# A fused threshold-attention and feed-forward kernel: input loads issued in smaller groups at round ends, and the first weight piece loaded and converted before the first scores

## The chip, the cores and the metric

The kernel runs on one core of one Trainium2 chip. The time is device microseconds (us) of one execution. Thirteen runs of the kernel before gave a median of 927.81 us, from 918.07 to 934.68.

## The reference

Two blocks follow each other. The first is attention with a threshold, for 8 batches of 8 heads, 576 tokens, head size 64:

```python
scores = scale * np.matmul(q, k.transpose(0, 1, 3, 2))
thresh = np.max(scores, axis=-1, keepdims=True) - tau
scores = np.where(scores >= thresh, scores, -1000000000.0)
attn = np.exp(scores - np.max(scores, axis=-1, keepdims=True))
attn = attn / (np.sum(attn, axis=-1, keepdims=True) + 1e-09)
return np.matmul(attn, v)
```

Its output, with the heads side by side, is `x` of 4608 tokens by 512. The second block computes `h = x @ w_in` (1024 wide), `h * softmax(h)`, a layer norm over the 1024 with gain `g_ln`, and `@ w_out` back to 512. The weights come in as float64, so the kernel turns their 64-bit words into float32 itself.

## The kernel before, in words

**Rounds.** The work is one long list of 144 "slots" (`NS`), 18 for each batch (`PER`). A slot scores 128 queries against 576 keys for two heads. The main loop runs one round for each slot. In round s it issues the scores of slot s on PE (`scores`, L391), their thresholds on VectorE, here DVE (`maxes`, L408), the ramp and the exponential on ScalarE, here ACT (L419, L428), and for slot s-1 the normalising on GpSimd, POOL (L438), and the block transposes on DVE (`blocks`, L450). At each even round the transposed blocks of two slots go through four DMAs `wT<-T` (L461) into the layout that the product with v wants. That product (`attend`, L486) is issued three rounds after the second of the two slots (`LAG_PV`), so two rounds after its `wT<-T`.

**Feed-forward.** When a group of 128 tokens is complete, four of the later rounds carry its two halves of `x @ w_in` (`ff_h`, L540) and of `@ w_out` (`ff_o`, L642). Between these, `ff_swap` copies parts of `u` into `V` by four DMAs (L620), and `ff_turn` transposes V into `uT` on DVE (L630) one round later; `ff_o` needs `uT`.

**Loads.** q, k and v of a batch come in two halves of four heads. `load_qk` loads the half of q and k (512 KB each; the first half also the last 64 tokens of all heads, `ends`, 128 KB for q and for k), and `load_v` the half of v (1,152 KB in five DMAs). The table `load_at` says in which round each of these is issued, and the loop issues them at the round's start. For batch b, with r = 18(b-1): first q/k half in round r+2, second in r+8, first v half in r+9, second in r+24; for batch 1 the first three are in rounds 8, 12 and 15.

**Weights.** There are 16 pieces (`piece`, 8 of `w_in`, 8 of `w_out`) of 128x512 64-bit words, 512 KB. `weight_load` issues the DMA of a raw piece (L205), `weight_a` takes exponent and top bits apart (two DVE operations, L216 and L222, and one on ACT, L221), `weight_b` builds the float32 value (three DVE operations, L236, L239, L242), and `weight_d` swaps the halves of a `w_out` piece by two DMAs (L251). Piece x is finished (`weight_b`) at the end of round x, then the load of piece x+3 is issued, and `weight_a` of piece x+1 follows. There are three raw buffers.

**The preamble** issues q and k of the first half, tau, the constants, raw pieces 0 to 2 on ACT's queue, the second half of q and k, v, `whole_pair(0)` (the transposes L264 and their copies L297 to L342 for the first pair of heads) and `weight_a(0)`.

**Order.** The order on every engine is the order of the program text. Nearly all DMAs are issued by SyncE (SP) in that order, and an instruction that waits holds up all behind it. DMA completions are counted by eight semaphores, used in turn: a DMA that takes one over waits until its former user has landed.

Of the kernel before, what the change touches and what calls it, by code (L numbers as in the profile page):

```python
# [8 lines left out]
F32 = mybir.dt.float32  # L9
# [7 lines left out]
P = 128  # L17
# [3 lines left out]
def kernel(  # L21
# [27 lines left out]
    nc = tc.nc  # L49
    B, H, S, D = q.shape  # L50
    DM, DFF = w_in.shape
    SM = 512
# [7 lines left out]
    ROWS = (slice(0, 64), slice(64, P))  # L60

    const = ctx.enter_context(tc.tile_pool(name="const", bufs=1))
    loads = ctx.enter_context(tc.tile_pool(name="loads", bufs=2))
# [24 lines left out]
    NK = S // 64  # L88

    halves = {}  # L90
    ends = {}
# [8 lines left out]
    def take(name):  # L100
        tag = pairs_free.pop(0)
        return tag, ps_mm.tile([P, 1024], F32, tag=tag, name=name)
# [13 lines left out]
        )  # L116


    def load_qk(b, hf):
        d = halves.setdefault((b, hf), {})  # L120
        hs = slice(4 * hf, 4 * hf + 4)

        if hf == 0:
            ends[b] = loads.tile([P, H, D], F32, tag="ends", name="ends")
        for nm, src, rows in (("q", q, ROWS[0]), ("k", k, ROWS[1])):
            d[nm] = loads.tile([P, 4, 4, D], F32, tag=nm, name=nm)

            parts = [slice(0, 2), slice(2, 4)] if b == 0 and hf == 0 else [slice(0, 4)]
            for x, part in enumerate(parts):
                queue = nc.scalar if nm == "k" and x + 1 < len(parts) else nc.sync  # L130
                queue.dma_start(
                    out=d[nm][:, part].rearrange("p h t d -> p h (t d)"),
                    in_=src[b, hs, 0:SM, :][part].rearrange("h (p t) d -> p h (t d)", t=4),
                )
                if hf == 0 and x == 0:
                    queue.dma_start(
                        out=ends[b][rows], in_=src[b, :, SM:S, :].rearrange("h p d -> p h d")
                    )

    def load_v(b, hf):  # L140
        d = halves.setdefault((b, hf), {})
        hs = slice(4 * hf, 4 * hf + 4)


        d["v"] = loads.tile([P, 4, NK, D], F32, tag="v", bufs=3, name="v")
        rest = v[b, hs, 0:SM, :].rearrange("h (p t) d -> p h (t d)", t=4)
        for to, rows, of in (
            (0, slice(0, P), slice(0, P)), (4, ROWS[0], ROWS[1]), (4, ROWS[1], ROWS[0])
        ):
            nc.sync.dma_start(  # L150
                out=d["v"][rows, :, to : to + 4].rearrange("p h t d -> p h (t d)"), in_=rest[of]
            )
        for rows in ROWS:
            nc.sync.dma_start(
                out=d["v"][rows, :, NK - 1], in_=v[b, hs, SM:S, :].rearrange("h p d -> p h d")
            )

    def constants():

        nc.gpsimd.memset(lim, 0.0)  # L160
        nc.scalar.activation(out=ntau, in_=lim, func=AF.Exp)
        make_identity(nc, ident)
        nc.gpsimd.memset(mhalf, -0.5)
        nc.gpsimd.memset(mone, -1.0)
        nc.gpsimd.memset(lim, -896.0 * 8388608.0)

        nc.vector.tensor_scalar(
            out=scl, in0=tau_t, scalar1=0.0, scalar2=SCALE, op0=ALU.is_ge, op1=ALU.mult  # L170
        )
        nc.vector.tensor_scalar(
            out=tau_t, in0=tau_t, scalar1=0.0, scalar2=104.0, op0=ALU.max, op1=ALU.min
        )
        nc.vector.tensor_scalar(out=ntau, in0=tau_t, scalar1=-1.0, scalar2=None, op0=ALU.mult)
# [13 lines left out]
    def piece(x):  # L189
        if x < 2 * NP:  # L190
            c, hf = divmod(x, 2)
            cols = slice(512 * hf, 512 * hf + 512)
            return w_in[P * c : P * c + P, cols], w1[:, c, cols], W_UNIT
        c = x - 2 * NP
        return w_out[P * c : P * c + P], w2[:, 2 * c], gs[:, c : c + 1]

    NW = 2 * NP + NC
    raws = {}

    def weight_load(x):  # L200
        raw = work.tile(
            [P, 512], I64 if wide else F32, tag=("xh2", "xh3", "uT")[x % 3], bufs=1, name="raw"
        )
        queue = nc.scalar if x < 3 else nc.sync
        queue.dma_start(out=raw, in_=piece(x)[0])  # L205
        raws[x] = dict(raw=raw)

    def weight_a(x):
        if not wide:
            return  # L210
        d = raws[x]
        hi = d["raw"].bitcast(I32).rearrange("p (n two) -> p n two", two=2)[:, :, 1]
        d["em"] = e, m = [
            work.tile([P, 512], I32, tag=t, bufs=n, name="em") for t, n in (("ob", 2), ("xe", 1))
        ]
        nc.vector.tensor_scalar(  # L216
            out=e, in0=hi, scalar1=20, scalar2=0x7FF,
            op0=ALU.logical_shift_right, op1=ALU.bitwise_and,
        )

        nc.scalar.activation(out=e, in_=e, func=AF.Relu, bias=lim, scale=8388608.0)  # L221
        nc.vector.tensor_scalar(  # L222
            out=m, in0=hi, scalar1=0xFFFFF, scalar2=0x100000,
            op0=ALU.bitwise_and, op1=ALU.bitwise_or,
        )

    def weight_b(x):
        d = raws.pop(x)
        _, dst, unit = piece(x)
        if not wide:  # L230
            nc.vector.tensor_scalar(out=dst, in0=d["raw"], scalar1=unit, scalar2=None, op0=ALU.mult)
            return
        words = d["raw"].bitcast(I32).rearrange("p (n two) -> p n two", two=2)
        lo, hi = words[:, :, 0], words[:, :, 1]
        e, m = d["em"]
        nc.vector.scalar_tensor_tensor(  # L236
            out=dst, in0=lo.bitcast(U32), scalar=2.0**-32, in1=m, op0=ALU.mult, op1=ALU.add
        )
        nc.vector.scalar_tensor_tensor(  # L239
            out=e, in0=hi, scalar=-(2**31), in1=e, op0=ALU.bitwise_and, op1=ALU.bitwise_or  # L240
        )
        nc.vector.scalar_tensor_tensor(  # L242
            out=dst, in0=dst, scalar=unit, in1=e.bitcast(F32), op0=ALU.mult, op1=ALU.mult
        )
# [104 lines left out]
    def whole_pair(i):  # L349
        tags, tiles = zip(take("tp"), take("tp"))  # L350
        spare = dict(enumerate(tiles), base=0, eased=i > 0)
        items = [item(i) for item in (q_item, k_item, e_item)]
        for x, (_, make, _) in zip((0, 4, 8), items):
            make(spare, x)
        for x, (_, _, keep) in zip((0, 4, 8), items):
            for r in range(2):
                keep(spare, x, r)
        pairs_free.extend(tags)
# [317 lines left out]
    PER = NS // B  # L676
# [12 lines left out]
    for i in range(NP, NPAIR):  # L689
        b, hp = divmod(i, NP)  # L690
        at = 11 + 2 * hp if i < 2 * NP - 1 else PER * (b - 1) + (6 + 3 * hp if hp < 3 else PER - 1)
# [7 lines left out]
    load_at = {}  # L699
    for b in range(1, B):  # L700
        r = PER * (b - 1)

        for at, job, hf in zip(
            (2, 8, 9) if b > 1 else (8, 12, 15), (load_qk, load_qk, load_v), (0, 1, 0)
        ):
            load_at.setdefault(r + at, []).append(lambda b=b, job=job, hf=hf: job(b, hf))
        load_at.setdefault(r + PER + 6, []).append(lambda b=b: load_v(b, 1))

    with tc.manual_schedule():
        load_qk(0, 0)  # L710
        nc.scalar.dma_start(out=tau_t, in_=tau.partition_broadcast(P))
        constants()
        for x in range(3):
            weight_load(x)
        load_qk(0, 1)
        load_v(0, 0)
        nc.sync.dma_start(out=g_rows, in_=g_ln.rearrange("(c p) -> c p", p=P))
        whole_pair(0)
        weight_a(0)


        pieces = {r: x for x, r in enumerate(range(16))}
        whole = {0: 1, 2: 2, 4: 3}
        load_at[3] = [lambda: load_v(0, 1)]

        ready = []
        rnd = 0
# [7 lines left out]
        while True:  # L735
            more = rnd < NS
            if not more and not (
# [1 line left out]
                or max([rnd - 1, *begin, *middle, *late]) >= rnd  # L739
            ):  # L740
                break
            for job in load_at.pop(rnd, []):
                job()
            for job in begin.pop(rnd, []):
                job()
            if rnd == NS:
# [59 lines left out]
            elif step == ("h", 1):  # L806
# [8 lines left out]
                at = rnd + 4 if more or not ready else rnd + 6  # L815
# [16 lines left out]
            if attending is not None:  # L832
                attend(attending)
                attended(attending)
                b, kind, hp = attending
# [5 lines left out]
                blocks(rnd - 1)  # L841
            for job in late.pop(rnd, []):
                job()
            if rnd == 3:
                gains()
            if rnd in pieces:
                x = pieces[rnd]
                weight_b(x)
                if x + 3 < len(pieces):
                    weight_load(x + 3)  # L850
                if x + 1 < len(pieces):
                    weight_a(x + 1)
            if rnd - 1 in pieces:
                weight_d(pieces[rnd - 1])
# [35 lines left out]
```

## Time and profile before

| what | value |
|---|---|
| median of 13 runs | 927.81 us |
| the profiled execution, its own time | 923.17 us |
| its span in the profile | 921.4 us |
| PE busy | 851.0 us (92%) |
| DVE busy | 679.1 us (74%) |
| ACT busy | 591.7 us (64%) |
| POOL busy | 452.2 us (49%) |
| DMA queue q1 (SP's), share of 16 engines | 71.1% |
| PE waits in L486 for `wT<-T` | 8.2 us in 5 |
| DVE waits in L630 for `V<-u` | 24.8 us in 12 |
| DVE waits in L216 for raw pieces of `w_in` | 7.4 us in 4 |

The span is cut into stretches to see which engine is full where. A timeline row has its start, its duration, engine, line, operation, result<-sources, and, in brackets, how long the engine stood idle before it and who ended the wait. SPq and ACTq rows are the issue of DMAs, not their transfer. The trace lacks some of the matmul records, so a short gap on PE with the releaser "issue" need not be a wait.

### The profile page before, as it was taken

How to read it: one execution, taken by the hardware profiler on the slowest of the kernel's cores; microseconds unless marked ns; L12 is line 12 of the kernel's file. 1: busy time of each engine (PE TensorE's matmuls, PEld its weight loads, DVE VectorE, ACT ScalarE, POOL GpSimd, SP SyncE). 2: the span in 40 equal slices, each digit the busy share in tenths (PEclk: the TensorE clock that was granted, in tenths of full speed). 3: DMA queues.
4: the chain of work that ended last, by engine and by line, in shares of the span. 5: the costliest groups of instructions: out<-in, count | busy, mean ns of one | idle time of the engine just before them, and what ended most of it. 6: DMA issues, size and time to landing. Idle time of an engine off the chain costs nothing. (4 is left out here: it accounts for less than half of the span.)

```text
span 921.4 us, 39657 instructions
## 1 busy us (share of the span) xinstructions
PE 851.0 (92%) x17089; PEld 625.2 (68%) x17089; DVE 679.1 (74%) x1306; ACT 591.7 (64%) x1240; POOL 452.2 (49%) x870
## 2 busy tenths in 40 slices
PE   5567779989899999999999999989999999999997
PEld 3335457868676666767777667867767777887555
DVE  5898968768766777777777777777767777777351
ACT  5766667757656766667667766767757676766121
POOL 2544646536555455545555555545555555555120
PEclk8778799999999999999999999999999999999999
DMA  8899869975889557976889557975879555866412
GB/s 256 199 255 244 192 138 221 223 159 128 185 171 222 120 132 185 227 156 138 190 183 227 123 131 183 232 147 122 197 166 212 134 135 124 191 142 135 93 47 47
DMA packets 95470, 154.61 MB, mean 168 GB/s; under 512 B 27192, under 2 KB 69184, under 8 KB 95296
## 3 DMA queue, kind: packets, MB, share of 16 engines
q1 hardware_dynamic: 93920, 150.12, 71.1%
q8 instruction: 134, 2.20, 1.1%
q10 hardware_dynamic: 1376, 1.97, 0.6%
q14 instruction: 40, 0.33, 0.1%
HBM read 46.14 MB, written 9.44 MB: 60 GB/s over the span
## 5 line engine op out<-in xcount | busy, mean ns | idle before, releaser
L408 DVE CUSTOM_DVE_ANT_0 w<-s_ps,tau_t 128x576 f32<-128x576 f32 x288 | 206.5, 755 | 149.1 <-PE s_ps L391 125.4
L419 ACT ACTIVATE w<-s_ps,nth 128x576 f32<-128x576 f32 x288 | 207.4, 743 | 119.3 <-DVE nth L408 95.8
L642 PE MATMUL o_ps<-w,uT 64*64 64x256 f32 x4608 | 268.6, 376 | 6.9 <-DVE uT L630 6.6
L642 PEld LDWEIGHTS o_ps<-w,uT 64*64 64x64 f32 x4608 | 219.7, 133 | 63.9 <-issue 20.8
L438 POOL TENSOR_SCALAR w<-w,sm 128x576 f32<-128x576 f32 x288 | 218.4, 770 | 14.3
L540 PE MATMUL h_ps<-w,xh 64*64 64x512 f32 x1856 | 219.2, 590 | 3.6 <-issue 3.6
L428 ACT ACTIVATE w<-w,ntau 128x576 f32<-128x576 f32 x288 | 220.3, 772 | 0.0
L450 DVE STREAM_TRANSPOSE T<-w 128x576 f32<-128x576 f32 x288 | 205.9, 751 | 5.4 <-POOL w L438 4.2
L486 PEld LDWEIGHTS pv<-wT,v 64*64 64x64 f32 x5760 | 170.7, 138 | 46.9 <-issue 26.2
L391 PE MATMUL s_ps<-kT,qT 64*64 64x64 f32 (+1 forms) x2048 | 174.0, 423 | 22.1 <-ACT w L419 20.2
L486 PE MATMUL pv<-wT,v 64*64 64x128 f32 (+1 forms) x5760 | 174.7, 266 | 13.8 <-DMA wT<-T 8.2
L540 PEld LDWEIGHTS h_ps<-w,xh 64*64 64x64 f32 x1856 | 111.6, 133 | 94.3 <-issue 65.0
L435 POOL TENSOR_SCALAR sm<-sm 128x2 f32<-128x2 f32 x144 | 35.7, 248 | 277.7 <-ACT w L428 275.0
L436 POOL TENSOR_TENSOR sm<-sm,mone 128x2 f32<-128x2 f32 x144 | 107.1, 744 | 12.0
L391 PEld LDWEIGHTS s_ps<-kT,qT 64*64 64x64 f32 x2048 | 65.3, 138 | 35.0 <-ACT w L419 26.8
L604 ACT ACTIVATE V<-u,nb,rs 128x1024 f32<-128x1024 f32 x36 | 44.7, 1241 | 53.3 <-POOL nb L594 53.3
L508 ACT COPY xh<-pv 128x256 f32<-128x256 f32 x64 | 23.9, 373 | 74.3 <-PE pv L486 74.3
L630 DVE STREAM_TRANSPOSE uT<-V 128x1024 f32<-128x1024 f32 x36 | 44.1, 1224 | 24.9 <-DMA V<-u 24.8
L428 ACT ACTIVATION_READ_ACCUMULATOR w<-w,ntau 128x1 f32 x288 | 56.9, 198 | 0.0
L562 ACT ACTIVATE u<-h_ps,hm 128x1024 f32<-128x1024 f32 x36 | 40.2, 1118 | 24.4 <-DVE hm L553 18.3
L553 DVE TENSOR_REDUCE hm<-h_ps 128x1 f32<-128x1024 f32 x36 | 43.0, 1194 | 10.9 <-PE h_ps L530 5.5
L568 DVE TENSOR_TENSOR u<-h_ps,u 128x1024 f32<-128x1024 f32 x36 | 42.8, 1190 | 10.5 <-ACT u L562 10.5
(74 smaller groups left out, 604.5 us busy)
## 6 DMA issues: line engine op xcount, KB each, us to landing
wT<-T SPq DMA_DIRECT2D x288, 288.0 KB, 5.8
V<-u SPq DMA_DIRECT2D x144, 64.0 KB, 3.8
out_dram<-ob SPq DMA_DIRECT2D x72, 128.0 KB, 2.9
v<-in_v_dram SPq DMA_DIRECT2D x16, 512.0 KB, 9.0
v<-in_v_dram SPq DMA_DIRECT2D x32, 256.0 KB, 8.2
q<-in_q_dram SPq DMA_DIRECT2D x15, 512.0 KB, 6.1
k<-in_k_dram SPq DMA_DIRECT2D x15, 512.0 KB, 7.8
raw<-in_moe_w_out_dram SPq DMA_DIRECT2D x8, 512.0 KB, 9.4
```

The source lines that it names most:

```text
L391: nc.tensor.matmul(out=ps[h][ROWS[y], ks], lhsT=lhsT, rhs=d["kT"][ROWS[h], ks], start=True, stop=True,)
L408: nc.vector.tensor_tensor_reduce(out=w, in0=ps[:, 0:S], in1=tau_t.to_broadcast([P, S]), scale=1.0, scalar=BIG, op0=ALU.add, op1=ALU.min, a ...
L419: nc.scalar.activation(out=d["w"][x], in_=d["ps"][x][:, 0:S], func=AF.Prelu, bias=d["nth"][x], scale=-1.0, alpha=1.0e30,)
L428: nc.scalar.activation(out=w, in_=w, func=AF.Exp, bias=ntau, scale=1.0, accum_out=sm[:, x : x + 1])
L436: nc.gpsimd.tensor_tensor(out=sm, in0=sm, in1=mone, op=ALU.pow)
L438: nc.gpsimd.tensor_scalar(out=w, in0=w, scalar1=sm[:, x : x + 1], scalar2=1.0, op0=ALU.mult, op1=ALU.mult)
L450: nc.vector.transpose(out=T[:, :, r, h, :], in_=w)
L486: nc.tensor.matmul(out=to, lhsT=d["v"][ROWS[u], h0 + h, m ^ 4 * u if m < 8 else m], rhs=rhs, start=m == 0, stop=m == NK - 1,)
L540: mm = nc.tensor.matmul(out=h[ROWS[y], f], lhsT=x[ROWS[r], c, ROWS[y]], rhs=w1_parts[ROWS[r], c, part ^ r], start=part == 0 and c == 0, st ...
L604: nc.scalar.activation(out=V, in_=u, func=AF.Identity, bias=nb, scale=rs)
L630: nc.vector.transpose(out=uT, in_=d["V"].rearrange("p y (m x) -> p m y x", x=32))
L642: nc.tensor.matmul(out=d["o"][ROWS[z], 512 * r : 512 * r + 256], lhsT=d["uT"][ROWS[r], m].rearrange("p y x -> p (y x)"), rhs=w2[ROWS[r], m ...
```

## The change

- The rounds in which loads are issued, and their sizes. q and k of a half are issued apart (`load_one`), and v in two parts (512 KB, then 640 KB). For batch b > 1: q in round r-1, k in r+1, second half k in r+7 and q in r+9, first v half in r+11 and r+13, second in r+21 and r+23. For batch 1: k in 7, q in 8, k in 11, q in 12, v in 13 and 15, and the second v half in 21 and 23.
- Loads are issued at the end of a round (after `blocks` and the late jobs) in place of its start.
- Raw piece 0 is the first DMA on ACT's queue, ahead of k. `weight_a(0)` and `weight_b(0)` stand before the three small DVE operations on tau (`thresholds`, split from `constants`) and before `whole_pair(0)`. Then follow `weight_a(1)` and the load of piece 3.
- In round r, piece r+1 is finished in place of piece r. So rounds 0 to 14 carry pieces, and round 15 none.

The order of instructions on PE is the same in both programs, and so is POOL's. The core of the diff:

```diff
-    def load_qk(b, hf):
+    def load_one(b, hf, nm, queue=None):
...
+    def load_qk(b, hf):
+        load_one(b, hf, "q")
+        load_one(b, hf, "k")
+
+    def load_v(b, hf, parts=(0, 1, 2)):
...
+    def thresholds():
         nc.vector.tensor_scalar(
             out=scl, in0=tau_t, scalar1=0.0, scalar2=SCALE, op0=ALU.is_ge, op1=ALU.mult
         )
...
-        for at, job, hf in zip(
-            (2, 8, 9) if b > 1 else (8, 12, 15), (load_qk, load_qk, load_v), (0, 1, 0)
+        for at, job, hf, what in (
+            (-1 if b > 1 else 8, load_one, 0, "q"),
+            (1 if b > 1 else 7, load_one, 0, "k"),
+            (7 if b > 1 else 11, load_one, 1, "k"),
+            (9 if b > 1 else 12, load_one, 1, "q"),
+            (11 if b > 1 else 13, load_v, 0, (0,)),
+            (13 if b > 1 else 15, load_v, 0, (1, 2)),
+            (PER + 3, load_v, 1, (0,)),
+            (PER + 5, load_v, 1, (1, 2)),
         ):
...
-        load_at.setdefault(r + PER + 6, []).append(lambda b=b: load_v(b, 1))
 
     with tc.manual_schedule():
+        weight_load(0)
         load_qk(0, 0)
         nc.scalar.dma_start(out=tau_t, in_=tau.partition_broadcast(P))
         constants()
-        for x in range(3):
+        for x in range(1, 3):
             weight_load(x)
...
+        weight_a(0)
+        weight_b(0)
+        thresholds()
         whole_pair(0)
-        weight_a(0)
-        pieces = {r: x for x, r in enumerate(range(16))}
+        weight_a(1)
+        weight_load(3)
+        pieces = {r: r + 1 for r in range(NW - 1)}
...
-            for job in load_at.pop(rnd, []):
-                job()
             for job in begin.pop(rnd, []):
...
             for job in late.pop(rnd, []):
                 job()
+            for job in load_at.pop(rnd, []):
+                job()
...
                 weight_b(x)
-                if x + 3 < len(pieces):
+                if x + 3 < NW:
                     weight_load(x + 3)
-                if x + 1 < len(pieces):
+                if x + 1 < NW:
                     weight_a(x + 1)
```

## Prediction

> **What bounds the kernel now.** I first cut the span into stretches, because the busy shares (PE 92%, DVE 74%) average over stages with different limits. Columns: stretch, its length, then busy us of PE, PE weight loads, DVE, ACT, POOL with instruction counts, granted PE clock, DMA share, GB/s.
>
> ```profile
> 22.00:27.50 5.50, 3.08 (x84) 1.93 (x76) 5.36 (x12) 5.05 (x13) 3.59 (x6) 0.90 0.52 122
> 44.00:49.50 5.50, 0.83 (x8) 0.29 (x4) 2.95 (x8) 2.14 (x4) 1.51 (x3) 0.77 1.03 225
> 66.00:71.50 5.50, 1.51 (x16) 0.35 (x14) 5.46 (x12) 3.82 (x8) 2.97 (x4) 0.63 1.03 240
> 104.50:110.00 5.50, 5.50 (x106) 3.81 (x102) 5.47 (x12) 5.19 (x13) 3.92 (x6) 0.95 0.94 202
> 605.00:610.50 5.50, 2.32 (x41) 1.65 (x40) 3.28 (x5) 0.89 (x1) 1.08 (x2) 1.00 0.62 111
> ```
>
> There are two stages. Up to about 104 us DVE is full in most stretches (5.36 and 5.46 of 5.50) and PE is not: a round takes about 5.5 us of DVE, because every round carries a weight piece. Where DVE is not full (44 to 49.5), DMA is: share 1.03. From 104 us on PE is full almost everywhere, so only PE's own gaps count there. The busy-time table gives 851.0 of 921.4 us to PE; of the 70 us of gaps, 47 lie before 138 us.
>
> Next I read the waits and, in order of time, the rows in which the loads and weight pieces take part.
>
> ```profile
> 4.67 2.46 ACTq L205 DMA_DIRECT2D raw<-in_moe_w_in_dram  x3
> 7.24 0.47 ACT L297 ACTIVATE qT<-tp,scl 128x256 f32<-128x256 f32 x1 [3.12 <-PE tp L264]
> 11.84 0.43 DVE L216 TENSOR_SCALAR em<-raw 128x512 int32<-128x512 int32 x1 [3.57 <-DMA raw<-in_moe_w_in_dram]
> 12.52 0.75 DVE L408 CUSTOM_DVE_ANT_0 w<-s_ps,tau_t 128x576 f32<-128x576 f32 x1
> 17.04 0.36 SPq L717 DMA_DIRECT2D g_rows<-in_moe_g_ln_dram  x1
> 46.55 0.43 DVE L216 TENSOR_SCALAR em<-raw 128x512 int32<-128x512 int32 x1 [3.07 <-DMA raw<-in_moe_w_in_dram]
> 72.77 0.69 PE L486 MATMUL pv<-wT,v 64*64 64x128 f32 x4 [4.91 <-DMA wT<-T]
> 79.41 0.76 DVE L408 CUSTOM_DVE_ANT_0 w<-s_ps,tau_t 128x576 f32<-128x576 f32 x1 [2.47 <-PE s_ps L391]
> 109.68 2.24 SPq L150 DMA_DIRECT2D v<-in_v_dram  x3
> 118.96 1.25 DVE L630 STREAM_TRANSPOSE uT<-V 128x1024 f32<-128x1024 f32 x1 [4.11 <-DMA V<-u]
> 120.35 3.68 PE L642 MATMUL o_ps<-w,uT 64*64 64x256 f32 x64 [1.87 <-DVE uT L630]
> 607.22 1.25 DVE L630 STREAM_TRANSPOSE uT<-V 128x1024 f32<-128x1024 f32 x1 [4.84 <-DMA V<-u]
> 608.61 3.68 PE L642 MATMUL o_ps<-w,uT 64*64 64x256 f32 x64 [3.18 <-DVE uT L630]
> ```
>
> The first maxes (12.52) come right behind weight piece 0, which DVE waited 3.57 us for. At 72.77, 118.96 and 607.22 small transfers that PE needs arrive late because a block of loads was issued just ahead of them.
>
> **Part 1, the start: costs 2.9 us.** In the built program ACT's DMA issues wait on reused semaphores: before, the three raw issues waited for k, `ends` of k and tau; now raw pieces 1 and 2 wait for `ends` of q and for the second piece of q. The issues stand ahead of piece 0's ACT step and of the first qT. Before, `ends` of q landed at 1.23 + 5.4 = 6.6 and that q piece at 2.02 + 5.3 = 7.3. Raw 0 puts 512 KB in front; at the 354 GB/s of 5.5 to 11 us that is 1.5 us, of which I let the idle third of the DMA engines (share 0.65 in the first 5.5 us) take a third: 1.0. So raw 1 is issued at 7.6 and raw 2 at 8.3, and ACT runs its step (0.72) from 8.7 to 9.4. DVE then does L239 and L242 (0.68 + 0.69, to 10.8) and the tau operations; qT starts at about 11.1, not 7.24, and the scores end near 14.4. Next, `weight_a(1)` stands ahead of the first maxes. Raw 0 took 7.2 us from issue (4.67) to use (11.84); raw 1 with the same is there at 14.8, and 0.68 later the maxes start: 15.4 against 12.52, **+2.9**. If raw 1 is not the last and q's piece keeps its 7.3, scores end near 13.4 and it is +1.1; with the median 9.1 us of the raw landings it is +4.8. Piece 0's own 2.7 us on DVE are hidden only in part by DVE's old wait for tau (6.80 us).
>
> The Trainium skill (DMA: Bandwidth & Descriptors, "Queues, rings and completion order") says that each DMA engine takes one queue's descriptors in ring order, so k stands behind all of raw 0; at the page's 358 GB/s HBM limit an estimate gives 1.5 us, and the start would cost half a us more. No run here shows it yet; the row is k landing 3.9 us after issue.
>
> **Part 2, one piece less in round 15: worth 0.** In every round from 0 to 14 DVE still carries one `weight_a` and one `weight_b`. What goes is round 14's `weight_a` (0.67, from 105.20) and round 15's `weight_b` (2.0, from 109.38). PE runs without a gap from 104.31 to 118.48, and DVE then waits for it at 112.06, so PE covers both; without that cover it would be 2.7. Raw pieces keep their lead of two rounds, each issue now carrying the next index, so the 3.07 us at 46.55 stay. New is piece 3: SP reaches it only after g_rows, which waits for k (17.04), and DVE now wants it a round earlier, near 24.5. Issued at about 18.4 it has 6 us. The fastest raw landing was 3.7, the median 9.1, so 0 to +3; I take 0, since DMA share falls to 0.68 and 0.52 there.
>
> **Part 3, loads of batch 1: -2.4 and -1.9.** In round 8, q, k and both `ends` (1,280 KB) were issued from 57.5 to 60.7, just ahead of `wT<-T` (from 61.28) that PE waited for until 72.77. Now q and its `ends` (640 KB) go behind it: 655 kB at 275 GB/s is 2.4 us. The chain is pv, scores of round 11, maxes at 79.41; the weight piece of that round ends on DVE at 76.94, so at most 2.5 can go. **-2.4**. Late next would be `ends` of q, needed at about 76; issued near 66 with landings up to 8.1 it has about 2 us to spare. If it does not, the gain is 0. In round 15 five v DMAs (109.68 to 113.7) stood ahead of `V<-u` (113.79). Now 512 KB go two rounds earlier, and the rest behind `V<-u`, whose issue moves up 4 us; uT is then ready before PE is free at 118.48. **-1.9**, and up to -3.2 if the next gap (1.31 at 126.09) goes too.
>
> **Part 4, loads of batches 2 to 7: -3.7.** After 138 us PE waited for uT 3.18 us at 608.61 and 0.51 at 399.62, both with a 1,152 KB v block just ahead of `V<-u`. In the new order at most 640 KB stand there: 0.6 MB less at 230 GB/s is 2.2 to 2.7 us earlier, plus five issues of 0.6 us, which covers DVE's 4.84. So **-3.7**. The most is -9: all of DVE's other `V<-u` waits after 138 us are 16.6 in total, a third of which could be on PE's path. The other end is +3: now nearly every `wT<-T` has 512 or 640 KB ahead of it, where many had none. Their slack is two rounds (11 us) against a median landing of 5.8, largest 11.4. The v part in round r+21 waits on SP for the product that last reads the buffer; that ended at 248.4 in batch 2, where SP was free at 249, so this wait costs nothing.
>
> **Sum.** 2.9 + 0 - 2.4 - 1.9 - 3.7 = -5.1. Against the profiled execution's 923.17 that is 918.1. The median of the 13 runs stands 4.64 above that execution; with it the forecast is **922.7**.
>
> **Rivals.** *A, the gain is hidden or eaten:* PE's waits for uT differ between executions, and part 4 gives nothing; the start costs its 4.8. 4.8 - 2.4 - 1.9 = +0.5: 928.3. For it: after 138 us PE waits for all DMA together under 5 us. Against: the rows at 118.96 and 607.22 have a plain cause. *B, slower:* the first pieces come late. Raw 1 takes 9.1 us (+4.8) and raw 3, behind g_rows, also takes 9.1, which holds round 1 by 3; DVE is the bound to round 14, so all 7.8 reaches PE. With 1.9 back at round 17 and the rest hidden this is +5.9: 933.7. It decides once raw 3 lands more than 6 us after issue. For it: raw landings under load were 7.1 to 9.8 in the first 12 us. Against: after 16.5 us the DMA engines are half idle. *C, all uT waits go:* 2.9 - 2.5 - 3.2 - 9 = -11.8: 916.0. For it: DVE's 24.8 us of waits; against: PE felt 6.6 of them.
>
> **How the numbers follow.** Forecast case 0.46, A 0.27, B 0.17, C 0.10. A measurement of this kernel can tell about 0.5%, 4.6 us, from no change. The forecast case lies just beyond it (from -3 to -8 by its own bounds), so I count 0.40 of its 0.46 as faster and 0.06 as same, and with C faster is 0.50; A with the rest is 0.33 same; B is 0.17 slower. The range goes from C with 2 us to spare to B's neighbourhood: 914 to 933.
>
> **What would show it.** Start: first maxes near 15.4; near 12.5 or 18 would break part 1. Piece 3: no wait of L216's successor for raw in round 1. Round 10: PE's wait for `wT<-T` about 2.4 shorter, round 11's maxes no longer waiting for PE. Round 17: no wait of uT for `V<-u`. Later: the uT waits well under 24.8 in total, and no new waits of PE for `wT<-T`. The prediction is wrong if DVE's stage does not end within 3 us of before, or if PE's gaps after 138 us do not shrink.

## The result, and the profile after

The changed kernel took 911.27 us in the median of 11 runs (906.13 to 915.97), the kernel before 927.63 us in the 48 runs beside it (918.07 to 938.01). The ratio is 0.984 [0.981, 0.986]: 1.6% less time. The forecast of 922.7 had the right sign, but of the 16.4 us that went it named only 5.1, and the result lies below its range. The profiled execution took 910.56 us (span 908.8), so the profiled pair differs by 12.6 us. Ratios here and below compare runs beside each other on one chip and leave out executions in a slower state, so they need not be the quotient of the medians given.

The start first, in the changed kernel's timeline (columns as before):

```profile
5.31 0.43 DVE L220 TENSOR_SCALAR em<-raw 128x512 int32<-128x512 int32 x1 [5.31 <-DMA raw<-in_moe_w_in_dram]
...
7.67 1.69 ACTq L209 DMA_DIRECT2D raw<-in_moe_w_in_dram  x2
9.47 0.72 ACT L225 ACTIVATE em<-em,lim 128x512 int32<-128x512 int32 x1 [4.87 <-DMA q<-in_q_dram]
...
11.80 0.47 ACT L301 ACTIVATE qT<-tp,scl 128x256 f32<-128x256 f32 x1 [1.61 <-DVE scl L173]
...
14.68 0.43 DVE L220 TENSOR_SCALAR em<-raw 128x512 int32<-128x512 int32 x1 [1.74 <-DMA raw<-in_moe_w_in_dram]
...
15.36 0.75 DVE L412 CUSTOM_DVE_ANT_0 w<-s_ps,tau_t 128x576 f32<-128x576 f32 x1
```

The chain is the predicted one. Raw 1 and 2 are issued from 7.67, when a q piece has let ACT go (4.87 us of waiting). Piece 0's ACT step follows at 9.47, qT at 11.80, and the first maxes stand behind raw piece 1 at 15.36.

With the old start, DVE takes up tau when it lands, and that differs between executions. These are the rows of two profiles of the kernel before, first the one that the prediction read, then a second one (e0 below):

```profile
6.80 0.15 DVE L169 TENSOR_SCALAR scl<-tau_t 128x1 f32<-128x1 f32 x1 [6.80 <-DMA tau_t<-in_tau_dram]
8.43 0.15 DVE L169 TENSOR_SCALAR scl<-tau_t 128x1 f32<-128x1 f32 x1 [8.43 <-DMA tau_t<-in_tau_dram]
```

Over the eight profiles with the old start tau is taken up between 6.26 and 9.41, and the first maxes lie between 12.4 and 14.8. In the six with the new start DVE no longer waits for tau, and they lie between 15.3 and 15.6.

Round 10, round 11's maxes and round 17:

```profile
72.83 0.69 PE L490 MATMUL pv<-wT,v 64*64 64x128 f32 x4 [0.69 <-DMA wT<-T]
74.40 3.71 PE L490 MATMUL pv<-wT,v 64*64 64x128 f32 x66 [0.88 <-DMA wT<-T]
...
80.05 0.74 DVE L412 CUSTOM_DVE_ANT_0 w<-s_ps,tau_t 128x576 f32<-128x576 f32 x1
...
113.29 1.79 SPq L154 DMA_DIRECT2D v<-in_v_dram  x2
...
115.93 1.25 DVE L634 STREAM_TRANSPOSE uT<-V 128x1024 f32<-128x1024 f32 x1 [0.71 <-DMA V<-u]
...
118.58 3.72 PE L646 MATMUL o_ps<-w,uT 64*64 64x256 f32 x64
```

PE's wait of 4.91 for `wT<-T` is now 0.69 + 0.88. The rest of the v loads (113.29) stands behind `V<-u` (issued at 110.76), DVE waits 0.71 for it in place of 4.11, and PE's row at 118.58 has no wait.

The stretches that were shown of before, with the same columns:

```profile
22.00:27.50 5.50, 4.22 (x95) 3.16 (x95) 5.36 (x12) 4.26 (x9) 3.07 (x4) 0.69 0.33 113
44.00:49.50 5.50, 3.35 (x46) 1.80 (x38) 2.64 (x5) 2.02 (x6) 2.77 (x4) 0.72 1.04 237
66.00:71.50 5.50, 3.65 (x48) 1.64 (x40) 5.01 (x12) 3.65 (x8) 2.97 (x4) 0.81 0.90 191
104.50:110.00 5.50, 5.50 (x94) 3.56 (x92) 5.05 (x10) 4.62 (x12) 4.01 (x7) 0.94 0.85 186
605.00:610.50 5.50, 5.50 (x120) 4.78 (x116) 4.55 (x12) 4.32 (x8) 4.04 (x10) 1.00 0.36 50
```

In the first stage DVE or the DMA engines are as full as before (5.36; share 1.04). In the last row PE is full, where it had been busy 2.32 of 5.50; the changed kernel is over 9 us further on there. The product that had waited 3.18 us at 608.61 now has no wait:

```profile
599.31 3.79 PE L646 MATMUL o_ps<-w,uT 64*64 64x256 f32 x64
```

PE's longest waits between 138 and 890 us. The first list is the kernel before, the second the changed one (engine, line, what it waited for: us in total, times, longest):

```profile
PE s_ps L264 <- issue: 3.9, 4, 1.5
PE o_ps L642 <- DVE uT L630: 3.7, 2, 3.2
PE h_ps L540 <- issue: 3.6, 2, 2.0
PE pv L486 <- issue: 2.5, 5, 1.1
PE pv L486 <- ACT w L428: 1.4, 1, 1.4
```

```profile
PE h_ps L544 <- issue: 3.6, 3, 2.0
PE pv L490 <- DMA wT<-T: 2.3, 2, 2.1
PE s_ps L268 <- ACT qe L342: 0.9, 1, 0.9
PE s_ps L268 <- issue: 0.7, 2, 0.5
PE o_ps L646 <- issue: 0.7, 1, 0.7
PE s_ps L268 <- ACT w L423: 0.7, 2, 0.4
PE s_ps L395 <- ACT qT L301: 0.6, 1, 0.6
PE pv L490 <- issue: 0.4, 1, 0.4
```

The waits for uT are gone, as forecast. But the largest part of what went had the releaser "issue", which I had set aside as lost records, and a wait for `wT<-T`, 0.3 us before and 2.3 now, takes some back.

The time of the first maxes of each round, after minus before, places all this: +2.84 at round 0, +3.91 at round 10, +0.64 at 11, +0.63 at 14, +0.36 at 16, -2.35 at 17, -3.40 at 18 and 28, -12.45 at 143. It is no straight line: it moves where one execution had a wait that the other had not.

### The profile page after: what moved, and what is told of

Read it like the earlier page. It is cut to its first block, busy times and chain, and to the rows that moved or that the text cites. A ratio compares the mean times of both kernels' runs of the same rounds, so it can differ in the third digit from the quotient of the medians.

```text
span 908.8 us, 39662 instructions
## 1 busy us (share of the span) xinstructions
PE 850.5 (94%) x17089; PEld 656.7 (72%) x17089; DVE 680.1 (75%) x1306; ACT 591.9 (65%) x1240; POOL 452.0 (50%) x870
## 5 line engine op out<-in xcount | busy, mean ns | idle before, releaser
L646 PEld LDWEIGHTS o_ps<-w,uT 64*64 64x64 f32 x4608 | 231.9, 133 | 46.5 <-ACT xh L512 9.7
L490 PEld LDWEIGHTS pv<-wT,v 64*64 64x64 f32 x5760 | 174.1, 138 | 38.4 <-issue 16.9
L395 PE MATMUL s_ps<-kT,qT 64*64 64x512 f32 (+1 forms) x2048 | 175.6, 422 | 21.8 <-ACT w L423 17.8
L544 PEld LDWEIGHTS h_ps<-w,xh 64*64 64x64 f32 x1856 | 123.1, 133 | 83.0 <-issue 45.5
L395 PEld LDWEIGHTS s_ps<-kT,qT 64*64 64x64 f32 x2048 | 68.4, 138 | 30.1 <-ACT w L423 24.6
L634 DVE STREAM_TRANSPOSE uT<-V 128x1024 f32<-128x1024 f32 x36 | 44.0, 1221 | 10.5 <-DMA V<-u 10.3
```

The lines of the kernel that those rows point to most:

```text
L395: nc.tensor.matmul(out=ps[h][ROWS[y], ks], lhsT=lhsT, rhs=d["kT"][ROWS[h], ks], start=True, stop=True,)
L490: nc.tensor.matmul(out=to, lhsT=d["v"][ROWS[u], h0 + h, m ^ 4 * u if m < 8 else m], rhs=rhs, start=m == 0, stop=m == NK - 1,)
L544: mm = nc.tensor.matmul(out=h[ROWS[y], f], lhsT=x[ROWS[r], c, ROWS[y]], rhs=w1_parts[ROWS[r], c, part ^ r], start=part == 0 and c == 0, st ...
L634: nc.vector.transpose(out=uT, in_=d["V"].rearrange("p y (m x) -> p m y x", x=32))
L646: nc.tensor.matmul(out=d["o"][ROWS[z], 512 * r : 512 * r + 256], lhsT=d["uT"][ROWS[r], m].rearrange("p y x -> p (y x)"), rhs=w2[ROWS[r], m ...
```

## What the gaps "issue" are

I counted PE's instructions (matmuls and weight loads) up to each of its gaps. In every profile of this study the gaps of 0.25 us or more with the releaser "issue", between 104 and 890 us, lie a multiple of 254 counted instructions apart, to within 7. The exceptions are three gaps of 1.05 to 1.8 us, in front of a pv product near 190 us. The table of DMA queues says what has this period (queue, packets, MB, share of 16 engines; the changed kernel's page):

```profile
q1 hardware_dynamic: 93920, 150.12, 70.9%
q8 instruction: 134, 2.20, 1.1%
```

2.20 MB in 134 packets is 16.4 KB a packet, and PE's 34,178 instructions in 134 blocks are 255 a block: q8 brings PE's own instructions, one packet for each 254 or 255 of those that are counted. One gap of the changed kernel, and the DMA table of the one us in which its packet starts:

```profile
451.70 1.45 PE L544 MATMUL h_ps<-w,xh 64*64 64x512 f32 x8
455.14 1.09 PE L544 MATMUL h_ps<-w,xh 64*64 64x512 f32 x8 [1.99 <-issue]
```

```profile
q1 hardware_dynamic: 119, 0.17, 69.7%
q8 instruction: 1, 0.02, 7.1%
```

PE stops at 453.15 in the middle of a product. The packet starts at 452.61 and takes 1.14 us, so it is there at 453.75; PE goes on at 455.14, 1.39 us later. The traces hold the start and length of every packet. In all fourteen profiles the 99 gaps of this kind end 1.21 to 1.70 us after a packet has landed, while packets come 6 us apart: PE is waiting for its next block of instructions. The Trainium skill (Runtime: NRT & Kernel Launch, "Instruction fetch mechanics") gives the same blocks, 16 KiB for 256 instructions, fetched by a DMA queue of the sequencer, and calls the cost of a block boundary mostly hidden. Here 6 of some 125 boundaries between 104 and 890 us showed in the changed kernel, but the few cost 5.3 us, and 10.4 in the kernel before: more than all its waits for uT.

## The experiments

Two theories were on record. Theory S: small transfers that PE needs (`wT<-T`, `V<-u`) wait behind large blocks of loads. Theory F: PE's instruction blocks come late while large transfers run. In the table, "blocks" is the sum of PE's gaps at block boundaries, "uT" and "wT" its waits of 0.25 us or more for these, all in the profiled execution between 104 and 890 us. Each ratio is to the kernel before on the same chip, whose median was 925.65 us beside e1 to e4, 931.01 beside e5 to e7, and 926.92 beside e8 to e11.

| kernel | median us (runs) | ratio to before | blocks | uT | wT |
|---|---|---|---|---|---|
| before, two profiles | 927.63 (48) | 1 | 10.4; 11.5 | 5.6; 6.8 | 0.3; 0 |
| changed | 911.27 (11) | 0.984 [0.981, 0.986] | 5.3 | 0 | 2.3 |
| e1 loads alone | 910.82 (6) | 0.985 [0.980, 0.989] | 7.0 | 0 | 0 |
| e2 start alone | 935.92 (6) | 1.011 [1.005, 1.017] | 15.4 | 5.9 | 0 |
| e3 q and k split alone | 919.98 (12) | 0.997 [0.994, 1.000] | 7.8 | 7.3 | 0.3 |
| e4 v split alone | 914.77 (6) | 0.989 [0.984, 0.994] | 6.2 | 0 | 0.6 |
| e5 loads, early swap | 907.72 (6) | 0.978 [0.972, 0.984] | 3.0 | 0 | 2.6 |
| e7 e5 with finer loads | 909.31 (6) | 0.978 [0.974, 0.983] | 6.9 | 0 | 0.3 |
| e6 burst in the tail | 932.22 (1) | one run | 4.4 | 0 | 2.3 |
| e8 copies behind `V<-u` | 920.61 (10) | 0.994 [0.990, 0.998] | 8.4 | 0 | 6.3 |
| e9 copies ahead of `V<-u` | 983.23 (4) | 1.062 [1.056, 1.068] | 9.0 | 42.9 | 0 |
| e10 changed, again | 911.86 (6) | 0.985 [0.980, 0.989] | 8.8 | 0 | 1.2 |
| e11 e5, again | 907.94 (6) | 0.980 [0.975, 0.985] | 6.4 | 0 | 1.8 |

**One half alone.** e1 has the new load rounds, and the old preamble with piece r in round r:

```diff
-        weight_load(0)
         load_qk(0, 0)
...
-        weight_a(0)
-        weight_b(0)
-        thresholds()
         whole_pair(0)
-        weight_a(1)
-        weight_load(3)
-        pieces = {r: r + 1 for r in range(NW - 1)}
+        weight_a(0)
+        pieces = {r: r for r in range(NW)}
```

> The new load rounds with the old start (raw pieces behind k, piece 0 converted in round 0, 16 rounds with pieces). Theory S (small transfers queued behind big load blocks) and theory F (PE's instruction stream, which is itself fetched by DMA, comes late while big load blocks are moved) both say: the start's 2.84 us come back on top, so about 908.5, ratio 0.979; first maxes at 12.5, round 17 about 6 us earlier than before. Rival: the earlier pieces carry part of the gain; then 912 or more.

e2 is the other half: the new preamble, with the loads in their old rounds, at the round's start.

> The new start and the old load rounds, sizes and place. Theories S and F: slower by the start's 2.84 us and nothing else, about 930.5, ratio 1.003, first maxes near 15.4 and every later round about 2.8 us late up to round 14. Rival (the earlier pieces carry part of the gain): 927 or less.

e1 took as long as the whole change, and e2 was 1.1% slower than before. So the gain is the loads' part. But the start's 2.84 us did not come back in e1. Its first maxes are at +0.24, it is at -7.67 in round 18, and at -3.29 in round 19 (these differences are to the first profile of before). This is the row of e1's PE timeline:

```profile
125.02 1.55 PE L646 MATMUL o_ps<-w,uT 64*64 64x256 f32 x10 [2.39 <-DMA w<-w]
```

`ff_o` waits for the swap of the last `w_out` piece. With the old order of pieces that swap comes one round later, and once the loads hold nothing up in round 17 it is the next thing that PE lacks. One round earlier is worth what the early first piece costs.

e2 lost more than its start: +3.0 at round 0, +6.3 at round 22, +14.6 at round 143. Of this 5.0 is more waiting for instruction blocks (two gaps of 3.94 and 2.65 us), and from round 18 to 143 PE's own busy time is 7.0 us longer (705.2 against 698.2), at a mean granted clock of 0.959 over the span against 0.972. I had expected 2.8. The medians differ by 10.3 us as well, so the rest does not belong to this one execution alone; why it is there is open.

**Which loads.** In e3 only q and k come in the new rounds, v in one group in its old ones; in e4 only v is split. Both have the old start.

> Old start; only q and k get the new rounds, the v halves stay whole blocks of 1,152 KB in their old place. Theory S: the waits of uT for V<-u came behind v blocks, so they stay; only round 11's 3.3 us go: about 924, ratio 0.996. Theory F: every big block counts, q/k blocks of 1,024 and 1,280 KB as well, so about half of the remaining gain comes too: about 918, ratio 0.990, and gaps of PE with no releaser get fewer.

> Old start; only v gets the new rounds and parts, q and k of a half stay together in their old place. Theory S: all uT waits behind v blocks go, round 11's wait stays: about 912, ratio 0.983. Theory F: about half of the gain after round 17 stays away because the q/k blocks still hold up the instruction stream: about 917, ratio 0.989.

The waits for uT stay with the old v loads (7.3 us) and go with the split ones; in e4 the wait of round 10 stays instead:

```profile
73.38 0.69 PE L490 MATMUL pv<-wT,v 64*64 64x128 f32 x4 [5.48 <-DMA wT<-T]
```

In these waits theory S holds, with v as its larger half. The times do not decide: e3 stands at S's ratio (0.996), e4 at F's (0.989) and not at S's (0.983), which had in it the start's 2.84 us that e1 did not get either. The sums of block gaps are lower than before's in both.

**The early swap.** e5 is e1 with the swap in the round of its piece:

```diff
             if rnd in pieces:
+                weight_d(pieces[rnd])
...
-                weight_d(pieces[rnd - 1])
```

> The new load rounds with the old start (as in e1_loads_only), and the swap of a w_out piece issued in the same round in which the piece is finished, one round earlier. Theory T (the early first piece pays only because the last w_out pieces come a round earlier; with the old start PE waited 2.39 us for the swap w<-w at 125.02, and round 19 lost 4.4 us by it): the wait w<-w goes, the first stage ends about 4.4 us earlier than in e1_loads_only and 2.8 to 4.3 us earlier than in the changed kernel; time 906 to 908, ratio to before about 0.98. Rival: the swap is not what holds round 19, another wait (uT or wT) stands right behind it; no change against e1_loads_only, 910.8.

e7 has, besides, loads of 256 or 320 KB, about one in each round.

> As e5_swap_early, and for batches 1 on the loads in pieces of 256 or 320 KB, about one in each round. Theory S (small transfers wait behind large blocks of loads on the queue): the waits of PE for uT were gone already, DVE's fall from 5 us to about 2, PE's time does not change: same as e5_swap_early within 1 us. Theory F (PE's instruction stream is fetched by DMA in blocks of 256 instructions and comes late behind large transfers): the gaps of PE at multiples of 256 instructions, 5 to 7 us in the kernels with the new load rounds, fall to 2 to 4; 2 to 3 us less than e5_swap_early.

In e5 the wait `w<-w` is gone. Its profile has round 19 at -3.5 and the end at -15.2, with first maxes at +2.2, since tau landed late in that execution (DVE took it up at 9.41 us); a second one (e11 below) starts at +0.4 and has -7.4 and -16.0, so round 19 comes 4.1 us earlier than in e1, near the 4.4 forecast. e7 is a miss for both theories: not faster than e5, its block gaps 6.9 us against 3.0 and 6.4 in e5's two profiles, and DVE's waits for `V<-u` between 138 and 890 us 18.9 us in place of 5.3. With a load in nearly every round, nearly every `V<-u` has one ahead of it; PE felt 0.2 us of that.

e5 was then run beside the changed kernel on one chip:

> The changed kernel again, beside the next kernel and on the same chip, to compare the two: 906 to 916, ratio to before 0.984.

> The new load rounds with the old start and the earlier swap again, beside the changed kernel on the same chip. If the 4.7 us between their traces hold: ratio to before 0.977 to 0.98, 3 to 5 us under the changed kernel's median. Rival: the difference lies in the executions, and both have the same median within 1.5 us.

907.94 (904.66 to 909.20) stands against 911.86 (909.09 to 914.92): 3.9 us less, as their traces have it (4.3 at round 143). This version beats both kernels.

**More traffic.** e6 is the changed kernel with the last v half loaded again, unused, at the end of nine rounds of the tail.

> The changed kernel, and at the ends of nine rounds of the tail (after slot 143, about 840 to 897 us), where no loads run, the second v half of the last batch is loaded again (1,152 KB each time, into rotating buffers, its data not used). Theory F: PE, which has no gap of 0.25 us or more with the releaser 'issue' there in the changed kernel, gets some, and they fall at multiples of 256 PE instructions, 1 to 5 us in sum. Theory S alone: PE's new gaps have the releaser uT or V<-u only (up to 3 us each), and none with the releaser 'issue'.

PE's new waits are these, with no gap at a block boundary:

```profile
897.16 3.27 PE L646 MATMUL o_ps<-w,uT 64*64 64x256 f32 x28 [10.21 <-DVE uT L634]
...
915.88 9.84 PE L646 MATMUL o_ps<-w,uT 64*64 64x256 f32 x128 [9.75 <-DVE uT L634]
```

So S held, by three times more than I had put, and F's gaps did not come. The place tests F badly: only three packets fell into the burst, and each had over 11 us until PE needed it.

The same kernel as before, profiled a second time:

> The kernel before, unchanged, profiled a second time. Theory F: the gaps at multiples of 256 PE instructions lie elsewhere or have other lengths in this execution (10.4 us in sum in the first profile), and the sum of these gaps and of the uT waits (15.9 us) moves with the span. Rival (the gaps belong to the program, as a branch or a long instruction would): the same gaps at the same instructions with the same lengths.

Its block gaps are at other blocks, or have other lengths (2.57 us at 189.89 where the first had 0.94 at the same instruction, 2.38 at 716.38 where it had none, none where it had 1.54). So they are no property of an instruction. One boundary is steadier: the gap after some 16,700 instructions, near 453 us in the changed kernel, is there in every other kernel (1.2 to 2.3 us) and in neither profile of before.

e8 and e9 have 36 more copies of 512 KB, of no use to the output, in DRAM:

```diff
-    lambda t=cur: (ff_norm2(t), ff_swap(t))
+    lambda t=cur: (ff_norm2(t), ff_swap(t), reload())   # e8
+    lambda t=cur: (ff_norm2(t), reload(), ff_swap(t))   # e9
```

> The changed kernel with 36 more DMAs of 512 KB (a copy of part of k into a scratch in DRAM that nothing reads), each issued right behind the four V<-u of its group. Theory F (PE's instruction blocks come late when the DMA engines are busy): the sum of PE's gaps at multiples of 256 instructions rises from 5.3 us to 10 to 20 us, with no or few new waits for uT, since V<-u stands ahead of the copy; ratio to before 0.99 to 1.0. Theory S alone (only small transfers queued behind large ones cost time): only wT<-T, which follows, can be late, and it has two rounds of slack; time as the changed kernel, within 2 us.

> The same 36 copies, each issued right ahead of the four V<-u of its group. Theory S: V<-u lands about 2 us later in each of 36 groups, DVE's waits for it rise from 5 us to over 40 us, and PE waits for uT again, 5 to 30 us in sum; clearly slower than the run with the copies behind. Theory F: the gaps at multiples of 256 instructions are those of the run with the copies behind (10 to 20 us). If neither the place nor the traffic matters, both runs are as the changed kernel, 911.

PE's waits between 104 and 890 us, first with the copies behind, then with the copies ahead:

```profile
PE pv L500 <- DMA wT<-T: 6.3, 5, 3.6
PE h_ps L554 <- issue: 5.6, 3, 1.9
PE o_ps L656 <- issue: 2.1, 1, 2.1
```

```profile
PE o_ps L656 <- DVE uT L644: 42.9, 24, 3.5
PE h_ps L554 <- issue: 4.6, 3, 2.3
PE s_ps L405 <- issue: 2.4, 2, 1.7
```

Same bytes, same rounds: moved from behind four small DMAs to ahead of them they cost 62.6 us more. DVE's waits for `V<-u` between 138 and 890 us go from 9.6 to 101.8 us, PE's for uT from none to 42.9 (S had put 5 to 30), and L656's own time on PE grows from 272.4 to 279.7 us as the mean granted clock falls from 0.970 to 0.958. Behind, the copies still cost 8.8 us against the changed kernel on the same chip, where S had put at most 2; in the profiles 4.0 to 5.1 of it are waits for `wT<-T`, which comes next on the queue. F's forecast of 10 to 20 us failed in both: 8.4 and 9.0 are hardly above the changed kernel's 5.3 and 8.8. That PE waits for instruction blocks is shown; that mere traffic lengthens these waits is not.

The packets themselves say more than the gaps. For each packet the traces give its lag, from PE's passing of the block boundary before it to the packet's start, and q1's share of the DMA engines in the 3 us from that passing. Over all fourteen profiles the median lag is 0.1 us where the share is under 0.3, 0.8 from 0.3 to 0.6, 1.3 from 0.6 to 0.8, and 2.3 from 0.95 up. So packets start later where q1 is full, and PE stands only at the few whose lag is long. With v in one group (before, e0, e2, e3) the median lag at a share over 0.9 is 2.4 to 2.9 us, in all others 1.5 to 2.2. This goes together; no run sets the one and leaves the rest alone.

## Why the prediction was wrong

- **Start, +2.9: right, with some luck.** Measured +2.84, by the chain named. But the profile that it was measured against had tau early; against before's second profile it is +1.5. With the ring order that the prediction took from the Trainium skill it would have been 3.4. k did land behind raw 0 (6.93 us, raw 0 at 5.28), but the start waited last for raw piece 1. Unforeseen was that the order of pieces pays it back at round 19.
- **Piece 3, 0: right.** DVE waits for raw pieces of `w_in` only twice before 40 us, for piece 0 and piece 1; none in round 1.
- **One piece less in round 15, 0: right for the two steps named, wrong in what it left out.** Round 14 to 16 gave 0.3. The step listed which `weight_a` and `weight_b` go and what covers them, not what waits for the last swap. In e1 that is a wait of 2.39 us and 4.4 us at round 19.
- **Round 11, -2.4: right in the wait and in what limits it, but too small.** It should stand at 2.9 - 2.4 = +0.5, and stood at +0.64, behind the weight piece on DVE. That the two agree is luck: the start's 2.84 had grown to 3.91 by round 10, for a reason left open, and round 11 took back 3.27, more than the bound of 2.5.
- **Round 17, -1.9: too small.** From round 14 to 18 it was -4.0, past the -3.2 named as the most. Of the two waits of before there, uT 1.87 and the gap of 1.31 at 126.09, the second was a late instruction block, and both went; the other 0.8 was not traced. The row of before:

```profile
126.09 0.21 PE L264 MATMUL s_ps<-ident,q 64*64 64x64 f32 x1 [1.31 <-issue]
```

- **Part 4, -3.7: this term failed.** It measured -9.05, from round 28 to 143. Its own wait was exact: uT 3.18 + 0.51 = 3.7, all gone. Beside it, instruction blocks went from 9.1 to 5.3 us (-3.8), a wait of pv for ACT (-1.4) and a pv gap near 197 (-1.1) went, and `wT<-T` came in with +2.0, inside the +3 that was named. With +0.4 in waits for `w` that is -7.6. The last 1.5 is PE's own busy time between these rounds (646.3 against 644.8 us), with its cause open. I had taken "issue" for holes in the record, so the -3.8 had no term. Its size is partly that of one execution: e10 has 8.8 us of block gaps, and -7.1 over these rounds. Rival C (916.0) comes nearer in number, but not by what it named: its -9 here was uT waits alone, of which PE had 3.7 to lose.
- **From the profiled run to the median, +4.64: failed too.** The changed kernel's median stands 0.7 above its profiled run. So of the 11.4 us between forecast and median 7.5 is missing in the sum and 3.9 in this step. The step took the 4.64 for a constant that the change leaves alone. But before's second profile took 4.5 us more than its first: the first maxes came 1.4 later, as tau landed later, uT has 1.2 more and the blocks 1.1. The new start does not wait for tau, and the waits for uT are gone.

What stays open: why the new load rounds go with fewer late blocks. The three profiles with the old rounds have 10.4, 11.5 and 15.4 us, all others 3.0 to 9.0. Mere traffic (e8, e9) did not raise them clearly, and finer loads (e7) did not help. The longer lags with v in one group point to the size of the load blocks, but e3, which has them, has 7.8 us, so that is not shown.

## What to carry to other kernels

Ask of each load which small transfer stands behind it on the same queue and who needs that next: the same copies cost 8.8 us behind and over 70 ahead. When a step is moved by a round, follow it to its last reader, here the swap. And count the instructions between gaps that nothing explains before putting them down to the record.

## What the runs showed of the hardware

PE's instructions come by DMA in packets of 16.4 KB, one for each 254 or 255 that the profile counts, each of about 1.15 us, and PE can stand 0.3 to 3.9 us for one when it lands late; it goes on 1.2 to 1.7 us after the landing. In these kernels that was 3.0 to 15.4 us of an execution, and it moved between two executions of one program (5.3 and 8.8 us in the changed kernel). A packet's start lags more where the loads' queue is full: 0.1 us in the median under a share of 0.3, 2.3 us from 0.95 up.
